# Probabilities of the last query blocks turned by VectorE and placed by way of DRAM

## The chip, the cores and the metric

The kernel runs on one core of a Trainium2 chip. The metric is the device time of one execution in microseconds (us). The kernel before took 1031.83 us (median of three runs, 1031.17 to 1034.34). Engines: PE is TensorE (matmuls; PEld its weight loads), DVE is VectorE, ACT is ScalarE, POOL is GpSimd, SP is SyncE, which here only issues DMAs.

## The reference

Decay attention (4 batches, 8 heads, 576 tokens, head dimension 64, float32), then two feed-forward blocks over the 2304 tokens:

```python
scores = scale * q @ k.T                      # per batch and head, 576 x 576
cum = cumsum(log(clip(f, 1e-4, 1)))
scores = where(causal, -1e9, scores + cum[:, None] - cum[None, :])
attn = exp(scores - max(scores)); attn = attn / (sum(attn) + 1e-9)
x = (attn @ v)  -> (2304, 512)
h = x @ w_in;  x = maximum(0.01 * h, h) @ w_out          # 512 -> 2048 -> 512
out = ((x @ w_a) * (x @ w_b)) @ w_out2                   # 512 -> 1536 -> 512
```

## The kernel before

Tokens are cut into 9 chunks of 256 (`x_chunk`). For each chunk the first feed-forward block runs as eight pieces of `l1` (line 865) and `l2` (line 895); float32 is carried as a rounded high part and a low part, so that a product is three matmul passes. The remaining stages (from some 620 us on) are not touched by the change.

Attention is cut into eight blocks: batch b, and r = 0 for queries 0 to 255 or r = 1 for queries 256 to 575 against all 576 keys. `att_steps` emits block n beside the feed-forward work of chunk n - 1, and `tc.high_priority` lets its PE instructions go up to 300 places ahead; a planner then orders every engine's queue from its own costs, and the order is fixed when the program is built. A block's eight heads go by pairs; head j = 0 or 1 of pair hp.

For one head of an r = 1 block, `att_scores` does this: SP loads queries, keys and `cumb` (the decay row); POOL writes the decay and the causal mask into the probability tiles `p` (lines 390, 393), one of 384 and one of 512 columns for the two tiles of 128 queries; PE computes scores; DVE adds them and finds the row's extreme (line 402); ACT takes the exponential (line 373) and multiplies by the reciprocal of the sum (line 411). The 64 last queries of both heads form a tile of their own, `p4`.

`att_values` then turns the probabilities over, since the product with v needs keys on the partitions: 3 + 4 PE transposes of 128x128 into PSUM (`pp`, line 99 stands for every PE instruction of attention, being the helper that records them) and two ACT copies (line 500) into the tile `pt`, which has one buffer and holds both heads of a pair. The tiles `p` have two buffers per tag. `att_rest` does the same for `p4` (lines 540, 541, 548), and `att_product` multiplies: for each key tile kt and head u,

```python
q_ = (P if kt == nkt - 1 else 0) if kt < nkt else T1
pe_att.matmul(av[u * 64 : u * 64 + 64, q_:width], vn[:, kt, u, :], turned[kt][:, u, q_:width] ...)
```

so that the last full key tile, which only the second 128 queries see, skips the first 128 columns. Then ACT and DVE bring the result as high and low part into the chunks' tiles `xh` and `xl` (`evac`, lines 456, 457). The v rows `vn` are loaded by SP (lines 481, 483). In blocks with r = 0 and in batch 0 the same functions run with other sizes. `first_block` does block (0, 0) in an order written out by hand.

Of the kernel before, what the change touches and what calls it, by code (L numbers as in the profile page):

```python
# [8 lines left out]
F32 = mybir.dt.float32  # L9
# [5 lines left out]
ALU = mybir.AluOpType  # L15
# [3 lines left out]
P = 128  # L19
MASKED = 1.0e9  # L20
ABOVE = 3.0e38
# [5 lines left out]
def kernel(  # L27
# [13 lines left out]
    nc = tc.nc  # L41
    B, H, S, D = q.shape
# [211 lines left out]
    def x_chunk(c):  # L254
        if c not in xh:
            pool, bufs = (late["p"], 1) if c % 3 == 2 else (mp, 2)
            xh[c] = pool.tile([P, HP, T1], F32R, tag="xh", bufs=bufs, name=f"xh_{c}")
            xl[c] = pool.tile([P, HP, T1], F32R, tag="xl", bufs=bufs, name=f"xl_{c}")
        return xh[c], xl[c]

    x4, p4s, stats, qks, turned_p, vhls, phs, lasts, lastk = ({} for _ in range(9))

    def att_scores(b, r, h, st):
# [50 lines left out]
        else:  # L314
# [50 lines left out]
            q_at = lead + z0  # L365
        cumb = ap_.tile([P, S], F32, tag="cumb", bufs=3, name=f"cumb_{nm}")
        made = nc.sync.dma_start(cumb[:, :nk], cum_dram[bh : bh + 1, :nk].to_broadcast([P, nk]))
        if b == 0:
# [11 lines left out]
            return rec  # L380

        ps = st["ps"] = {}
        for i in range(2):
            t = 2 * r + i
            n = (t + 1) * P
            s = 2 * j + i
            pt = ap_.tile([P, 384 if i == 0 else 512], F32, tag=f"p{i}", bufs=2, name=f"p_{nm}_{t}")[:, :n]
            ps[i] = pt

            made = pool_att.tensor_scalar(pt, cumb[:, :n], 1.0, ncum_t[:, t, bh : bh + 1], op0=ALU.mult, op1=ALU.add)  # L390
            if (b, r, h) == (0, 1, 0):
                tc.add_manual_dep(made.ins, quiet[0].ins.name, SYNC, reason="second block's decay behind the fourth pair")
            pool_att.affine_select(
                out=pt[:, t * P : n], in_=pt[:, t * P : n], pattern=[[-1, P]], base=0,
                channel_multiplier=1, compare_op=ALU.is_ge, fill=MASKED,
            )
# [5 lines left out]
            dve_att.tensor_tensor_reduce(  # L402
                out=pt, in0=sp[:, :n], in1=pt, op0=ALU.add, op1=ALU.min, scale=1.0, scalar=ABOVE,
                accum_out=stat[:, 0, s : s + 1],
            )
            yield
            exp(pt, s)
            yield
# [46 lines left out]
    def evac(hi, lo, src):  # L455
        high = act_att.copy(hi, src)
        return high, dve_att.tensor_tensor(out=lo, in0=src, in1=f32(hi), op=ALU.subtract)


    def turned_tile(name):  # L460

        t = ap_.tile([P, 2688], F32, tag="pt", name=f"pt_{name}")
        return [t[:, 640 * kt : 640 * kt + 640].rearrange("p (u q) -> p u q", u=2) for kt in range(4)] + [
            t[:, 2560:].rearrange("p (u q) -> p u q", u=2),
            t,
        ]

    def att_values(b, r, h, st):

        hp, j = h // 2, h % 2  # L470
        nk = 2 * P if r == 0 else S
        tok0 = b * S + (0 if r == 0 else 2 * P)
        nm = f"{b}_{r}_{h}"
        pair = (b, r, hp)
        ps = st["ps"]
        if j == 0:
            turned_p[pair] = turned_tile(nm)
            full, rest = nk // P, nk % P
# [7 lines left out]
        turned = turned_p[pair]  # L486
        yield
        parts = [([(kt, 0) for kt in range(2 * r + 1)], 0), ([(kt, 1) for kt in range(2 * r + 2)], 1)]
        if r == 0:
            parts = [([(0, 0), (0, 1), (1, 1)], None)]  # L490
        for z, (tiles, i) in enumerate(parts):
            pp = ps_a.tile([P, 4, P], F32, tag="ps", bufs=3, name=f"pp_{nm}_{z}")
            for m, (kt, i_) in enumerate(tiles):
                pe_att.transpose(pp[:, m, :], ps[i_][:, kt * P : kt * P + P], ident)
            if i is None:
                act_att.copy(turned[0][:, j, 0:T1], pp[:, 0:2, :].rearrange("p m q -> p (m q)"))
                st["second"] = act_att.copy(turned[1][:, j, P:T1], pp[:, 2, :])
            else:
                to = turned[5][:, :2560].rearrange("p (k u q) -> p k u q", k=4, u=2)
                st["second"] = act_att.copy(to[:, : len(tiles), j, i * P : i * P + P], pp[:, : len(tiles), :])  # L500
            yield
        if r == 0:
            yield
        if j == 1 and (r == 0 or b == 0):
            yield from att_product(b, r, hp, st["second"])

    def att_product(b, r, hp, ready):

        pair = (b, r, hp)
        nm = f"{b}_{r}_{2 * hp}"  # L510
        turned, vn = turned_p[pair], vhls[pair]
        tok0 = b * S + 2 * P * r
        width = 320 if r and b else T1
        nkt = 2 * r + 2
        av = ps_a.tile([P, width], F32, tag="ps", bufs=3, name=f"av_{nm}")
        for kt in range(nkt + (width > T1)):
            q_ = (P if kt == nkt - 1 else 0) if kt < nkt else T1
            for u in range(2):
                made = pe_att.matmul(
                    av[u * 64 : u * 64 + 64, q_:width], vn[:, kt, u, :], turned[kt][:, u, q_:width] if kt < 4 else turned[4][:, u, :],  # L520
                    start=(kt == 0), stop=(kt == nkt - (width == T1)),
                )
                if kt == u == 0:
                    tc.add_manual_dep(made.ins, ready.ins.name, SYNC, reason="both heads at once")
        p0 = 0
        while p0 < width:
            c = (tok0 + p0) // T1
            c0 = tok0 + p0 - c * T1
            n = min(width - p0, T1 - c0)
            ch, cl = x_chunk(c)  # L530
            evac(ch[:, hp, c0 : c0 + n], cl[:, hp, c0 : c0 + n], av[:, p0 : p0 + n])
            p0 += n
        yield

    def att_rest(b, hp, rec4):

        pair = (b, 1, hp)
        nm = f"{b}_1_{2 * hp}"
        turned, p4 = turned_p[pair], p4s[b, hp]
        act_att.mul(p4, p4, rec4)  # L540
        nc.gpsimd.memset(turned[5][64:, 2560:], 0.0)
        main = turned[5][:, :2560].rearrange("p (k u q) -> p k u q", k=4, u=2)[:, :, :, T1:320]
        tail = turned[5][:, 2560:].rearrange("p (k u q) -> p k u q", k=1, u=2)
        for k0, k1, w, to in ((4, 5, S - 4 * P, tail), (0, 4, P, main)):
            pp = ps_a.tile([P, 4, P], F32, tag="ps", bufs=3, name=f"pp{k1}_{nm}")
            for kt in range(k0, k1):
                pe_att.transpose(pp[:w, kt - k0, :], p4[:, kt * P : kt * P + w], ident)
            ready = act_att.copy(to[:w], pp[:w, : k1 - k0, :].rearrange("p k (u q) -> p k u q", u=2))
            yield
        yield from att_product(b, 1, hp, ready)  # L550

    def att_last(b, hp, rec4):
# [2 lines left out]
        vhl = vhls[b, 1, hp]  # L555

        p4 = p4s[b, hp]
        ph = turned_tile(f"4_{nm}")[5][:, :640].rearrange("p (k q) -> p k q", k=5)
# [63 lines left out]
    def first_block():  # L622
# [128 lines left out]
                )  # L751

        def probs(p, j, i):
            both = tile_of(
                ("p", p, j), lambda: ap_.tile([P, 384], F32, tag="qll" if p == 2 else f"p{j}", bufs=2, name=f"p_f{p}_{j}")
            )
            return both[:, i * P : i * P + (i + 1) * P]

        def D(p, j, i):
# [50 lines left out]
                pe.transpose(pp[:, z, :], probs(p, j, i)[:, kt * P : kt * P + P], ident)  # L810

        def h(p, j):
            pt = tile_of(("pt", p), lambda: turned_tile(f"f{p}")[5])
# [648 lines left out]
```

## Time and profile before

| | |
|---|---|
| median of 3 runs | 1031.83 us |
| the profiled execution | 1030.66 us |
| its span, first to last instruction | 1028.9 us |
| PE, DVE, ACT, POOL busy | 98%, 65%, 54%, 17% of the span |
| granted TensorE clock, mean | 0.992 |

The profile is one execution taken by the hardware profiler. Busy time is the union of an engine's instruction records; matmul records overlap, and their ends are modelled, so a matmul's cost is read from the distance of starts rather than from its length. The chain of waits follows the work that ended last back from instruction to instruction, through what released each.

### The profile page before, as it was taken

How to read it: one execution, taken by the hardware profiler on the slowest of the kernel's cores; microseconds unless marked ns; L12 is line 12 of the kernel's file. 1: busy time of each engine (PE TensorE's matmuls, PEld its weight loads, DVE VectorE, ACT ScalarE, POOL GpSimd, SP SyncE). 2: the span in 40 equal slices, each digit the busy share in tenths (PEclk: the TensorE clock that was granted, in tenths of full speed). 3: DMA queues.
4: the chain of work that ended last, by engine and by line, in shares of the span. 5: the costliest groups of instructions: out<-in, count | busy, mean ns of one | idle time of the engine just before them, and what ended most of it. 6: DMA issues, size and time to landing. Idle time of an engine off the chain costs nothing.

```text
span 1028.9 us, 19822 instructions
## 1 busy us (share of the span) xinstructions
PE 1005.5 (98%) x7299; PEld 913.8 (89%) x7299; DVE 671.6 (65%) x1383; ACT 557.9 (54%) x1144; POOL 178.4 (17%) x402
## 2 busy tenths in 40 slices
PE   6899999999999999999999999999999999899998
PEld 5677779999999999999999997888888888799998
DVE  5799656755626555264367547668686675898872
ACT  6688687986748867488455444232322222354430
POOL 3525325442413324133000000000000000000000
PEclk9899999999999999999999999999999999999999
DMA  8997145543532436321583123233151423757711
GB/s 218 270 266 217 48 96 110 106 93 62 112 78 62 92 62 110 80 55 45 188 298 119 62 62 103 94 122 118 57 164 41 159 100 125 238 150 203 212 53 42
DMA packets 230497, 125.78 MB, mean 122 GB/s; under 512 B 144704, under 2 KB 212160, under 8 KB 230400
## 3 DMA queue, kind: packets, MB, share of 16 engines
q1 hardware_dynamic: 224784, 118.67, 42.0%
q10 hardware_dynamic: 5616, 5.84, 1.7%
q8 instruction: 58, 0.95, 0.4%
q14 instruction: 39, 0.32, 0.1%
HBM read 95.29 MB, written 29.17 MB: 121 GB/s over the span
## 4 chain that ended last, share of the span: by engine, by line
PE 92%; DMA 4%; ACT 1%; DVE 1%; POOL 1%; issue 1%; SPq 0%; ACTq 0%; POOLq 0%; DVEq 0%
PE h L865 19%; PE y L895 19%; PE o L1200 12%; PE s L99 6%; PE b_b L1090 5%; PE b_a L1090 5%; PE av L99 5%; PE pp L99 4%; PE a_a L1090 3%; PE a_b L1090 3%; PE d_b L1090 3%; PE d_a L1090 3%; DMA homef<-in_moe_w_out_dram 2%; PE a_last L1122 2%; PE b_last L1122 2%; DMA homef<-o_dram 1%
## 5 line engine op out<-in xcount | busy, mean ns | idle before, releaser
L895 PE MATMUL y<-gh,homer 128*128 128x256 f32 x1152 | 227.2, 284 | 0.6 <-ACT gh L877 0.6
L865 PE MATMUL h<-xh,homer 128*128 128x256 f32 x1152 | 225.6, 283 | 0.9 <-ACT hs L878 0.9
L865 PEld LDWEIGHTS h<-xh,homer 128*128 128x128 f32 x1152 | 183.4, 188 | 5.6 <-issue 2.7
L895 PEld LDWEIGHTS y<-gh,homer 128*128 128x128 f32 x1152 | 183.8, 188 | 3.8 <-issue 2.1
L895 PE MATMUL y<-gl,homer 128*128 128x256 f32 x576 | 162.5, 284 | 0.0
L865 PE MATMUL h<-xl,homer 128*128 128x256 f32 x576 | 161.6, 281 | 0.0
L895 PEld LDWEIGHTS y<-gl,homer 128*128 128x128 f32 x576 | 108.4, 188 | 1.1 <-issue 0.9
L865 PEld LDWEIGHTS h<-xl,homer 128*128 128x128 f32 x576 | 108.3, 188 | 0.5
L390 POOL TENSOR_SCALAR p<-cumb,ncum_t 128x384 f32<-128x384 f32 (+2 forms) x112 | 75.7, 679 | 149.3 <-PE pp L99 86.3
L880 DVE TENSOR_TENSOR gl<-hs,gh 128x512 fp32r<-128x512 f32 x72 | 50.9, 707 | 71.9 <-ACT hs L878 71.3
L373 ACT ACTIVATE p<-p,stat 128x256 f32<-128x256 f32 (+3 forms) x123 | 73.6, 600 | 36.0 <-DVE stat L402 30.7
L402 DVE CUSTOM_DVE_ANT_0 p<-s,p 128x384 f32<-128x384 f32 (+2 forms) x100 | 48.4, 491 | 39.6 <-PE s L99 29.8
L877 ACT ACTIVATE gh<-h 128x512 fp32r<-128x512 f32 x72 | 42.7, 593 | 41.7 <-PE h L865 40.9
L411 ACT ACTIVATE p<-p,rec 128x384 f32<-128x384 f32 (+1 forms) x108 | 56.1, 572 | 11.5 <-DVE rec L379 10.6
L99 PE MATMUL pp<-ident,p 128*128 128x128 f32 (+1 forms) x376 | 62.2, 276 | 0.0
L1200 PE MATMUL o<-homer,homer 128*128 128x256 f32 x441 | 57.7, 284 | 0.0
L1200 PEld LDWEIGHTS o<-homer,homer 128*128 128x128 f32 x441 | 55.2, 191 | 0.2
L1200 PE MATMUL o<-w_o,homer 128*128 128x256 f32 x378 | 52.6, 284 | 1.4 <-ACT homer L933 1.4
L933 ACT CAST homer<-p 128x1536 fp32r<-128x1536 f32 (+1 forms) x26 | 33.7, 1320 | 35.3 <-DVE p L958 20.4
L1200 PEld LDWEIGHTS o<-w_o,homer 128*128 128x128 f32 x378 | 48.6, 191 | 2.1 <-ACT homer L933 1.8
L99 PEld LDWEIGHTS pp<-ident,p 128*128 128x128 f32 (+1 forms) x376 | 43.4, 139 | 4.0 <-issue 2.3
L99 PE MATMUL av<-pt,vn 128*64 128x320 f32 (+4 forms) x400 | 46.9, 372 | 0.0
(272 smaller groups left out, 2047.6 us busy)
## 6 DMA issues: line engine op xcount, KB each, us to landing
p<-p_dram SPq DMA_DIRECT2D x17, 768.0 KB, 6.6
p_dram<-p SPq DMA_DIRECT2D x12, 1024.0 KB, 4.3
cumb<-cum_dram SPq DMA_DIRECT2D x32, 288.0 KB, 3.9
homef<-in_moe_w_out_dram SPq DMA_DIRECT2D x15, 511.6 KB, 6.0
homef<-in_moe_w_in_dram SPq DMA_DIRECT2D x15, 510.5 KB, 4.7
raw_o<-in_moe_w_out_dram SPq DMA_DIRECT2D x12, 511.6 KB, 5.9
xq<-in_q_dram SPq DMA_DIRECT2D x144, 32.0 KB, 2.1
y_dram<-yo ACTq DMA_DIRECT2D x18, 256.0 KB, 2.9
```

The lines of the kernel that those rows point to most:

```text
L99: return method(*args, **kw)
L373: act_att.activation(pt, pt, AF.Exp, bias=stat[:, 0, s : s + 1], scale=-1.0, accum_out=stat[:, 1, s : s + 1])
L390: made = pool_att.tensor_scalar(pt, cumb[:, :n], 1.0, ncum_t[:, t, bh : bh + 1], op0=ALU.mult, op1=ALU.add)
L402: dve_att.tensor_tensor_reduce(out=pt, in0=sp[:, :n], in1=pt, op0=ALU.add, op1=ALU.min, scale=1.0, scalar=ABOVE, accum_out=stat[:, 0, s : ...
L411: act_att.mul(ps[i], ps[i], rec[:, i : i + 1])
L865: made = nc.tensor.matmul(hps[:, u, :], w[:, c * P : c * P + P], x[:, c, :], start=(n == 0), stop=(n == 3 * ND - 1))
L877: nc.scalar.activation(gh, hps, AF.Prelu, alpha=0.01)
L880: nc.vector.tensor_tensor(out=gl, in0=hs, in1=f32(gh), op=ALU.subtract)
L895: nc.tensor.matmul(o, w[:, d * P : d * P + P], g[:, u, :], start=(fi == 0 and n == 0 and d % 2 == 0), stop=(fi == NF1 - 1 and n == 2 and d ...
L1090: nc.tensor.matmul(to, w[:, W_ROWS[m], wl, c2 * P : c2 * P + P], y[c2][xl_][:, Y_COLS[m], :], start=(first and c2 == e == 0), stop=(c2 == ...
L1122: nc.tensor.matmul(ps[:, f * T1 : f * T1 + T1], w[:, wb, wl, c2 * P : c2 * P + P], y[:, xb, xl_, c2 * T1 : c2 * T1 + T1], start=(f == m == ...
L1200: nc.tensor.matmul(ps[m], xps[n, j // 3][:, X_ROWS[m], xl_, j % 3, :], wo2[j][:, O_COLS[m], wl, :], start=(j == e == y == 0), stop=(j == N ...
```

## The change

In blocks with b > 0 and r = 1 (`turns_by_dma`) PE's transposes and ACT's copies go. Both query tiles of a head share one tile `p` of 1024 columns, in which 32-column pieces of the first and the second tile alternate; POOL writes zeros where the first tile has no fourth key tile. One DVE instruction transposes every 32x32 block of it in place. Four DMAs on SP (one per 32 partitions) store it to a buffer in DRAM (`turn_dram`, one per parity of hp), in runs of 256 bytes; four DMAs load it from there into `pt` in runs of 1 KB, keys on the partitions. The queries come out regrouped: 32 of the first tile, 32 of the second, and so on. So the product's last full key tile covers all columns (zeros included), and `evac` picks its sources by 32s and writes each query tile and the 64 last queries apart. Elsewhere the tiles `p` of the two query tiles become one tile of 1024 columns with two buffers, `pt` is laid out head by head, and the two loads of the last v rows become one.

```diff
+    turn_dram = [dram.tile([32, 2, 4, 4, T1], F32, name=f"turn_{z}_dram") for z in range(2)]
+    VIA_DRAM = (0, 1)
+    def turns_by_dma(b, r, j):
+        return b > 0 and r == 1 and j in VIA_DRAM
...
+        both = ap_.tile([P, 1024], F32, tag="p", bufs=2, name=f"p_{nm}")
+        if turns_by_dma(b, r, j):
+            st["both"] = both
+            both = both.rearrange("p (c t k) -> p c t k", t=2, k=32)
+            pool_att.memset(both[:, 12:, 0, :], 0.0)
         for i in range(2):
...
-            pt = ap_.tile([P, 384 if i == 0 else 512], F32, tag=f"p{i}", bufs=2, name=f"p_{nm}_{t}")[:, :n]
+            if turns_by_dma(b, r, j):
+                blocks_of = lambda ap: ap.rearrange("p (c k) -> p c k", k=32)
+                pt, diagonal, pattern = both[:, : n // 32, i, :], both[:, 4 * t : 4 * t + 4, i, :], [[-32, 4], [-1, 32]]
+            else:
+                blocks_of = lambda ap: ap
+                pt = both[:, i * (n - P) : i * (n - P) + n]
+                diagonal, pattern = pt[:, t * P : n], [[-1, P]]
...
     def turned_tile(name):
         t = ap_.tile([P, 2688], F32, tag="pt", name=f"pt_{name}")
+        main, tail = t[:, :2560].rearrange("p (u k q) -> p u k q", u=2, k=4), t[:, 2560:].rearrange("p (u q) -> p u q", u=2)
+        return main, tail, t
...
-                if rest:
-                    nc.sync.dma_start(vs[:rest, full, u, :], v[b, h + u, full * P : nk, :])
             if rest:
+                nc.sync.dma_start(vs[:rest, full, :, :], v[b, h : h + 2, full * P : nk, :].rearrange("u p d -> p u d"))
...
+        if turns_by_dma(b, r, j):
+            both, turn = st["both"], turn_dram[hp % 2][:, j]
+            dve_att.transpose(out=both, in_=both)
+            for z in range(4):
+                nc.sync.dma_start(
+                    turn[..., 64 * z : 64 * z + 64].rearrange("j k b q -> j (k b) q"),
+                    both[32 * z : 32 * z + 32, :].rearrange("p (c q) -> p c q", c=16),
+                )
+            yield
+            for z in range(4):
+                nc.sync.dma_start(main[32 * z : 32 * z + 32, j, :, :T1], turn[:, :, z])
+            yield
+            return
...
-        for kt in range(nkt + (width > T1)):
-            q_ = (P if kt == nkt - 1 else 0) if kt < nkt else T1
+        wide = width > T1
+        for kt in range(nkt + wide):
+            q_ = T1 if kt == nkt else P if kt == nkt - 1 and not wide else 0
...
+        runs = [(0, T1, av)]
+        if wide:
+            tiles = av[:, :T1].rearrange("p (a t q) -> p t a q", t=2, q=32)
+            runs = [(t * P, t * P + P, tiles[:, t]) for t in range(2)] + [(T1, width, av[:, T1:].rearrange("p (a q) -> p a q", q=32))]
+        for p0, p1, src in runs:
+            while p0 < p1:
...
+                    evac(hi, lo, src[:, first_ : first_ + n // 32, :])
```

## Rows read from the trace of the kernel before

**Rows 1.** The page: engine, busy us (share of span) and instructions; the chain's shares.
```profile
PE 1005.5 (98%) x7299; PEld 913.8 (89%) x7299; DVE 671.6 (65%) x1383; ACT 557.9 (54%) x1144; POOL 178.4 (17%) x402
...
PE 92%; DMA 4%; ACT 1%; DVE 1%; POOL 1%; issue 1%; SPq 0%; ACTq 0%; POOLq 0%; DVEq 0%
```

**Rows 2.** Busy time by stretch: bounds, length; PE, PEld, DVE, ACT, POOL busy (instructions); clock.
```profile
160.00:510.00 350.00, 349.37 (x2909) 329.73 (x2908) 182.61 (x559) 252.09 (x631) 115.64 (x288) 1.00 0.39 86
```

**Rows 3.** Stretch 160 to 510 us: the chain by line; PE's waits (us, times, longest).
```profile
by line: PE h L865 33.7%; PE y L895 33.0%; PE s L99 11.1%; PE av L99 9.6%; PE pp L99 9.3%; DMA cumb<-cum_dram 2.1%; POOL p L418 0.6%; issue 0.5%; POOL p L393 0.1%; POOL p L390 0.1%; DVE stat L402 0.0%; POOL p L424 0.0%; POOL qhh L335 0.0%; 
...
PE s L99 <- DVE stat L402: 0.6, 1, 0.6
```

**Rows 4.** Timeline of PE from 449.9 us: start, length, line, operation, tiles, count.
```profile
449.95 2.28 PE L99 MATMUL av<-pt,vn 128*64 128x320 f32 x20
452.16 0.98 PE L99 MATMUL pp<-ident,p 128*128 128x128 f32 x7
452.90 0.38 PE L99 MATMUL s<-ks,qhh 128*128 128x288 f32 x1
453.12 0.30 PE L99 MATMUL s<-ks,qll 128*128 128x288 f32 x1
```

**Rows 5.** Instruction groups by shape, 160 to 510 us: busy us, mean ns; idle before.
```profile
L99 PE MATMUL av<-pt,vn 128*64 128x192 f32 x48 | 5.9, 326 | 0.0
```

**Rows 6.** The same view, DVE's transpositions.
```profile
L326 DVE STREAM_TRANSPOSE tq<-xq 128x320 f32<-128x320 f32 x24 | 12.2, 510 | 0.6
...
L350 DVE STREAM_TRANSPOSE tk<-xk 128x576 f32<-128x576 f32 x11 | 8.3, 756 | 0.0
```

**Rows 7.** The same view, the copy out of PSUM and the low part's subtraction.
```profile
L500 ACT COPY pt<-pp 128x512 f32<-128x512 f32 x24 | 14.1, 588 | 0.4 <-PE pp L99 0.4
...
L457 DVE TENSOR_TENSOR xl<-av,xh 128x128 fp32r<-128x128 f32 x16 | 4.5, 290 | 11.5 <-ACT xh L456 11.4
```

**Rows 8.** Timeline of ACT, POOL and PE around two pairs' ends.
```profile
355.62 1.24 ACT L411 ACTIVATE p<-p,rec 128x384 f32<-128x384 f32 x2
...
367.68 1.03 PE L99 MATMUL av<-pt,vn 128*64 128x320 f32 x6
...
462.22 1.23 ACT L411 ACTIVATE p<-p,rec 128x384 f32<-128x384 f32 x2
...
466.61 2.28 PE L99 MATMUL av<-pt,vn 128*64 128x320 f32 x20
...
468.75 1.23 ACT L411 ACTIVATE p<-p,rec 128x384 f32<-128x384 f32 x2 [0.49 <-DVE rec L379]
...
469.53 1.27 POOL L390 TENSOR_SCALAR p<-cumb,ncum_t 128x384 f32<-128x384 f32 x2
...
483.91 2.28 PE L99 MATMUL av<-pt,vn 128*64 128x320 f32 x20
```

**Rows 9.** DMAs: issue on SP (ns, min/median/max), landing; KB and median landing.
```profile
L481 SPq DMA_DIRECT2D vn<-in_v_dram x56: 368/462/1138, 41.2 to 470.3; - x56
...
DMA to landing us min/median/max: 1.9/2.4/6.4
...
vn<-in_v_dram SPq DMA_DIRECT2D x32, 128.0 KB, 2.5
ty<-y_dram SPq DMA_DIRECT2D x16, 256.0 KB, 3.0
...
vn<-in_v_dram SPq DMA_DIRECT2D x24, 64.0 KB, 2.1
```

**Rows 10.** Timeline of SP, first and last of 22 issues of one pair.
```profile
198.28 0.38 SPq L481 DMA_DIRECT2D vn<-in_v_dram  x1
...
209.11 0.42 SPq L345 DMA_DIRECT2D xk<-in_k_dram  x1
```

**Rows 11.** Batch 3's last product (timeline); the `h` matmuls issued before 524.25 us.
```profile
497.33 2.28 PE L99 MATMUL av<-pt,vn 128*64 128x320 f32 x20
...
L865 PE MATMUL h<-xh,homer x896: 274/280/390, 44.1 to 524.2; 128*128 128x256 f32 x180
```

More of the change, by code (lines that the diff above doesn't have):

```diff
@@ L363, in score @@
                 pe_att.matmul(o, qll[:, c0 : c0 + P], ks[:, cols_], start=False, stop=True)
[L365 removed]
+            q_at = 2 * z0
         cumb = ap_.tile([P, S], F32, tag="cumb", bufs=3, name=f"cumb_{nm}")
@@ L386, in att_scores @@
             s = 2 * j + i
-            pt = ap_.tile([P, 384 if i == 0 else 512], F32, tag=f"p{i}", bufs=2, name=f"p_{nm}_{t}")[:, :n]
+            if turns_by_dma(b, r, j):
[5 more added lines that the diff above has]
+                diagonal, pattern = pt[:, t * P : n], [[-1, P]]
             ps[i] = pt
-            made = pool_att.tensor_scalar(pt, cumb[:, :n], 1.0, ncum_t[:, t, bh : bh + 1], op0=ALU.mult, op1=ALU.add)
+            made = pool_att.tensor_scalar(
+                pt, blocks_of(cumb[:, :n]), 1.0, ncum_t[:, t, bh : bh + 1], op0=ALU.mult, op1=ALU.add
+            )
             if (b, r, h) == (0, 1, 0):
@@ L393, in att_scores @@
             pool_att.affine_select(
-                out=pt[:, t * P : n], in_=pt[:, t * P : n], pattern=[[-1, P]], base=0,
+                out=diagonal, in_=diagonal, pattern=pattern, base=0,
                 channel_multiplier=1, compare_op=ALU.is_ge, fill=MASKED,
@@ L402, in att_scores @@
             dve_att.tensor_tensor_reduce(
-                out=pt, in0=sp[:, :n], in1=pt, op0=ALU.add, op1=ALU.min, scale=1.0, scalar=ABOVE,
+                out=pt, in0=blocks_of(sp[:, :n]), in1=pt, op0=ALU.add, op1=ALU.min, scale=1.0, scalar=ABOVE,
                 accum_out=stat[:, 0, s : s + 1],
@@ L490, in att_values @@
             parts = [([(0, 0), (0, 1), (1, 1)], None)]
+        if mixed:
+            ordered = main[:, j, :, :T1].rearrange("p k (z t q) -> p k z t q", z=4, t=2)
+            nc.gpsimd.memset(ordered[:, 3, :, 0, :], 0.0)
         for z, (tiles, i) in enumerate(parts):
@@ L510, in att_product @@
         nm = f"{b}_{r}_{2 * hp}"
-        turned, vn = turned_p[pair], vhls[pair]
+        (main, tail, _), vn = turned_p[pair], vhls[pair]
         tok0 = b * S + 2 * P * r
@@ L524, in att_product @@
                     tc.add_manual_dep(made.ins, ready.ins.name, SYNC, reason="both heads at once")
[L525 to L532, printed above, removed]
+        runs = [(0, T1, av)]
[4 more added lines that the diff above has]
+            while p0 < p1:
+                c = (tok0 + p0) // T1
+                c0 = tok0 + p0 - c * T1
+                n = min(p1 - p0, T1 - c0)
+                hi, lo = (x[:, hp, c0 : c0 + n] for x in x_chunk(c))
+                if wide:
+                    first_ = (p0 % P) // 32
+                    hi, lo = (x.rearrange("p (a q) -> p a q", q=32) for x in (hi, lo))
+                    evac(hi, lo, src[:, first_ : first_ + n // 32, :])
+                else:
+                    evac(hi, lo, src[:, p0 : p0 + n])
+                p0 += n
         yield
@@ L540, in att_rest @@
         act_att.mul(p4, p4, rec4)
[L541 to L544, printed above, removed]
+        nc.gpsimd.memset(turned[2][64:, 2560:], 0.0)
+        for k0, k1, w, to in (
+            (4, 5, S - 4 * P, turned[1].rearrange("p u (k q) -> p k u q", k=1)),
+            (0, 4, P, turned[0][..., T1:320].rearrange("p u k q -> p k u q")),
+        ):
             pp = ps_a.tile([P, 4, P], F32, tag="ps", bufs=3, name=f"pp{k1}_{nm}")
@@ L753, in probs @@
         def probs(p, j, i):
-            both = tile_of(
-                ("p", p, j), lambda: ap_.tile([P, 384], F32, tag="qll" if p == 2 else f"p{j}", bufs=2, name=f"p_f{p}_{j}")
-            )
+            if p == 2:
+                both = tile_of(("p", p, j), lambda: ap_.tile([P, 384], F32, tag="qll", bufs=2, name=f"p_f{p}_{j}"))
+            else:
+                both = tile_of(("p", p), lambda: ap_.tile([P, 1024], F32, tag="p", bufs=2, name=f"p_f{p}"))
+                both = both[:, j * 512 : j * 512 + 384]
             return both[:, i * P : i * P + (i + 1) * P]
```

27 lines of the change are left out of this document (14 added, 13 removed).

## The prediction

> **What bounds the kernel now.** I read the busy table and the chain of waits first [rows 1]. TensorE (PE) is busy 1005.5 of 1028.9 us and the chain that ended last runs on it for 92% of the span: what leaves PE's queue leaves the time, as long as nothing makes PE wait in its place. Since shares of busy time are averages over stages, I looked at the stretch that the change edits, the attention of batches 1 to 3. There PE is busy 349.37 of 350 us at a granted clock of 1.00, while VectorE (DVE) has 183 us of work, ScalarE (ACT) 252 and GpSimd (POOL) 116 [rows 2]. Its own chain says what that PE time is: two thirds MoE matmuls, 9.3% the `pp` transposes; and 2.1% of it passes through the transfer of `cumb`, which ends in the one PE wait of the stretch, 0.6 us [rows 3]. So attention runs beside MoE work, which fills PE, and a transpose costs exactly its own PE time.
>
> **What is removed from PE.** A head has 3 + 4 transposes in `att_values`; with 8 heads and 3 batches that is 168. The matmul records (270 ns) overlap, so I don't multiply by them. Seven transposes start at 452.16 and the next matmul at 452.90, with a record longer than its like by 0.08: 0.82 us, 0.118 each [rows 4]. Over the whole stretch the chain gives 9.3% of 350 us, 32.6 us, to 288 transposes, 0.113 each [rows 3]. I take the mean over many, 0.113: 168 x 0.113 = 19.0 us (0.118 gives 19.8).
>
> A rule of the Trainium skill speaks against the change: VectorE: DVE Perf Modes, "Rules for kernel authors", wants a 128x128 transpose on TensorE when its result may lie in PSUM, as here; the same page's "The three transpose paths" gives it 390 ns. By that figure 65 us would leave PE and the sum would be about 970 us, an estimate; the rows show the pitch, and the pitch decides.
>
> **What is added to PE.** With queries regrouped, the product's fourth key tile can no longer skip its first 128 columns: 192 columns become 320. A pair's product is 20 matmuls, 2.21 us [rows 4]: 12 of 320 columns, 4 of 192 [rows 5], 4 of 64, 4864 columns, 0.45 ns each. 4 x 128 more make 0.23 us, for 12 pairs 2.8 us.
>
> **What is added elsewhere.** DVE: the transposition of 128x1024 a head. Rows of 320 and 576 elements took 510 and 756 ns [rows 6], 0.96 ns an element, so 1.18 us, and 24 heads 28.4 us on an engine with 183 of 350 us in use: it hides. ACT loses two copies a head, of 512 columns (588 ns [rows 7]) and of 384, some 25 us in all. The results now leave PSUM in 4, 3 and 4 pieces a pair (batches 1, 2, 3) instead of 2: 20 more copies and subtractions, about 0.29 us each [rows 7], 6 us on ACT and on DVE, not in front of PE. POOL gets a small memset a head. The probabilities' two halves now share a buffer, so the first half comes free only with the second, half a microsecond later than now (four of the seven transposes of [rows 4]).
>
> **The way through DRAM, beside the path.** Per head: 1.2 us DVE, four stores, four loads. The nearest row to a store of 128 KB in runs of 256 B is the load of `vn`, same size and runs: 0.46 us of SP each and 2.5 us to landing; to the reload (runs of 1 KB) it is `ty`, 3.0 us [rows 9]. Stores: 3 x 0.46 + 2.5 = 3.9; reloads: 3 x 0.46 + 3.0 = 4.4; together 9.5 us. Bounds: 8 us if all land in the 1.9 us of the quickest, 17 if in the 6.4 us of the slowest [rows 9]. I take 9.5, by the rows of the same size and runs.
>
> What hides it? In the pair whose second head is normalised by 469.98 (468.75 + 1.23), the product starts at 483.91, 13.9 us later, since the 64 last queries go through scores, exponential and their own transposes meanwhile [rows 8]. So the second head's reload has 4.4 us to spare; in the shortest of the twelve pairs (356.86 to 367.68) it has 1.3. At the upper bound of 17 us PE would wait 3.1 us or more in each of twelve products, 37 us. The first head, done by 463.45, lets go of its buffer at 469.53 now, and would after its stores at 463.45 + 5.1 = 468.6 [rows 8]; its reload must wait for the product of the pair before (466.61 to 468.8), because `pt` has one buffer, and then stands in SP's queue ahead of the next pair's loads. The cadence of 16.7 us a pair survives.
>
> A second rule of the skill, DMA: Bandwidth & Descriptors, "Specifications", has transfers below 512 B done as read-modify-write. No run here shows it for stores. Were it to double the data time (2.5 less 2.1 us for 64 KB more in [rows 9], so 0.8 a store), four stores would take 3.2 us more: 12.7 us, still under 13.9 and the sum unchanged, but over the shortest pair's 10.8. It adds a little to the first rival's chance.
>
> **SP's queue** is the tight place. A loaded pair has 22 issues from 198.28 to 209.53 [rows 10], 9.9 us by their durations. The change adds 16 and takes 1 away (`vs` in one transfer instead of two): 15 x 0.46 = 6.9, so 16.8 us in a pair of 16.7. In SP's queue every load stands behind a store that waits for DVE, or a reload that waits 2.5 us for the stores to land. But there is room: only the first three pairs of a block carry the next heads' loads, and the results are needed late. The last product of batch 3 ends at 499.6, and the first chunk that reads it starts with the L865 matmuls after 524.2 (by then 896 = 7 chunks x 128 of the `xh` kind are issued) [rows 11]: 24.7 us, 19 once the block's own PE work shrinks by 5.7.
>
> **Sum.** 1030.66 (the profiled execution; 1.2 us under the median of the runs, so within their scatter) - 19.0 + 2.8 = 1014.5. For twelve new places where PE can wait I add 1.5 us, between none and twelve times the 0.6 us of the one wait that PE has there now [rows 3]. 1016 us.
>
> **Rivals.**
> 1. SP falls behind and PE waits for the products (slower). If nothing fills the two landing waits of a pair, SP needs 16.8 + 5.0 = 21.8 us for 16.7: 5.1 late a pair, piling up over the three loaded pairs of a block, less the spare 4.4: 10.9 us of PE standing still at the last product, in the blocks of batches 1 and 2 (batch 3 has few loads left): 1016 + 21.8 = 1038. It decides from 14.5 us of waiting in all, 1.2 a product. For it: SP is full already, the chain's 2.1% through `cumb`. Against: 24.7 us of slack behind a block, loads that can run in the landing waits.
> 2. PE's order is fixed ahead by the planner. Where it counts on a shorter way through DRAM than 9.5 us, products stand too early in PE's queue, every one of them. At 1 us each, twelve take 12 us: 1028, within 0.3% of before. For it: no row shows what the planner takes a transfer to cost, and a PE without idle time has no cover against its errors. Against: the 4.4 us to spare.
> 3. Nothing is gained because PE had idle time there: excluded by 349.37 of 350 us [rows 2].
>
> **Chances.** Forecast 0.66 (1009 to 1022); rival 2 at 0.15 (1022 to 1031); rival 1 at 0.18 (1031 and more); 0.01 below. A measurement of this kernel tells about 0.3%, 3.1 us, from no change. Faster by more: 0.66, 0.01 and half of rival 2, 0.74; within: 0.08; slower: 0.18. The range 1009 to 1036 leaves out rival 1's upper part.
>
> **What would show it.** PE has 168 `pp` instructions fewer, and no products of 192 columns. PE stays at full in 160 to 500, and attention's last product lies some 15 us earlier than 497.3 or a little less. Right: no idle time of PE before `av`; stores land 2 to 3 us after issue. Wrong: PE waits for `pt` from a DMA, in the products of batches 1 and 2 more than in batch 3 (rival 1) or in all alike (rival 2); SP's queue without gaps; `cumb` waited for by POOL for longer.

## The result and the profile after

The changed kernel takes 1047.16 us (median of 4 runs) against 1031.92 beside it: ratio 1.0148, 95% interval 1.012 to 1.0177. It is slower by some 1.5%, and outside the predicted range. The first profiled execution took 1050.55 us, a second one 1043.66.

The page of the changed kernel, as in [rows 1]: busy time, the busiest DMA queue, and the chain.

```profile
PE 1004.7 (96%) x7131; PEld 904.6 (86%) x7131; DVE 698.6 (67%) x1427; ACT 538.7 (51%) x1116; POOL 176.7 (17%) x426
...
q1 hardware_dynamic: 289040, 143.85, 52.7%
...
PE 71%; DMA 10%; SPq 7%; ACT 3%; issue 3%; DVE 3%; POOL 2%; POOLq 0%; ACTq 0%; DVEq 0%
```

The 168 transposes are gone (7299 to 7131 matmuls), but the chain has left PE: 92% to 71%, with 10% DMA and 7% SP's queue (SPq) in it. The same stretch as [rows 2] and the head of its chain, as [rows 3]:

```profile
160.00:510.00 350.00, 335.81 (x2686) 309.87 (x2685) 209.85 (x611) 232.60 (x615) 120.57 (x326) 1.00 0.70 147
```

```profile
by line: PE h L917 17.5%; PE y L947 16.1%; PE s L100 6.3%; PE av L100 6.2%; SPq L329 5.1%; DMA xk<-in_k_dram 4.9%; DMA turn_dram<-p 4.5%; issue 4.3%; SPq L512 3.8%; SPq L518 2.9%; DMA pt<-turn_dram 2.8%; SPq L352 2.3%; ACT p L432 1.8%; POOL
```

PE is idle for 14 of 350 us where it was idle for 0.6, and DMA's share (next to last in the row) went from 0.39 to 0.70. The chain now passes through the stores (L512), the reloads (L518), and also through the loads of queries (L329) and keys (L352) behind them in SP's queue. PE's waits in the attention of batches 1 to 3 (us in total, times, longest):

```profile
PE av L100 <- DMA pt<-turn_dram: 5.1, 4, 2.7
PE s L100 <- DVE stat L423: 4.1, 6, 1.6
PE y L947 <- ACT gh L929: 1.8, 1, 1.8
PE s L100 <- ACT qhh L344: 1.6, 1, 1.6
```

Only a third is products waiting for `pt`; the scores wait too. Queries and keys come late: VectorE, which transposes them, waits for their loads (140 to 560 us), as it never did before:

```profile
DVE tq L333 <- DMA xq<-in_q_dram: 13.3, 12, 3.0
DVE tk L357 <- DMA xk<-in_k_dram: 7.9, 7, 2.0
```

SP's queue shows why (start, length, issues); from 245 to 270 us no two of its rows are more than 0.2 us apart:

```profile
245.03 2.19 SPq L518 DMA_DIRECT2D pt<-turn_dram  x3
247.26 0.92 SPq L329 DMA_DIRECT2D xq<-in_q_dram  x2
248.22 0.45 SPq L352 DMA_DIRECT2D xk<-in_k_dram  x1
248.78 2.26 SPq L512 DMA_DIRECT2D turn_dram<-p  x4
251.09 1.89 SPq L352 DMA_DIRECT2D xk<-in_k_dram  x3
...
254.12 1.74 SPq L518 DMA_DIRECT2D pt<-turn_dram  x4
255.97 2.45 SPq L512 DMA_DIRECT2D turn_dram<-p  x4
258.45 2.04 SPq L329 DMA_DIRECT2D xq<-in_q_dram  x3
```

Stores and reloads stand between the loads, four and four, at 0.44 to 0.73 us each; they land a little later than the 2.5 and 3.0 us of the prediction (issue to landing, median):

```profile
turn_dram<-p SPq DMA_DIRECT2D x96, 128.0 KB, 3.0
pt<-turn_dram SPq DMA_DIRECT2D x96, 128.0 KB, 3.2
```

**A ruler.** To compare stages I use the first `h` matmul of each chunk: from chunk 1 to chunk 7 (or 8) lies all attention of batches 1 to 3. Before, that is 140.0 to 524.3: 384.2 us (431.6 to chunk 8). After: 392.5 and 391.8 in the two executions (439.9 and 439.7). So the stage lost 8 us instead of gaining 15. Where distances between successive starts of matmuls exceed 0.33 us, I add up what exceeds 0.12 ("excess"): 2.0 us before, 20.5 and 20.8 after. The granted clock matters to this ruler: in the stage the records have it at 0.5 (1.2 GHz) for no time in the kernel before and in the first execution of the changed one, but for 6.8 us in the second. The rest of the difference in the first pair of profiled executions, 12 us, lies ahead of chunk 1, which starts at 152.0 instead of 140.0.

### The profile page after: what moved, and what is told of

It is laid out like the page before. It is cut to its first block, busy times and chain, and to the rows that moved or that the text cites. A ratio compares the mean times of both kernels' runs of the same rounds, so it can differ in the third digit from the quotient of the medians.

```text
span 1048.8 us, 19858 instructions
## 1 busy us (share of the span) xinstructions
PE 1004.7 (96%) x7131; PEld 904.6 (86%) x7131; DVE 698.6 (67%) x1427; ACT 538.7 (51%) x1116; POOL 176.7 (17%) x426
## 4 chain that ended last, share of the span: by engine, by line
PE 71%; DMA 10%; SPq 7%; ACT 3%; issue 3%; DVE 3%; POOL 2%; POOLq 0%; ACTq 0%; DVEq 0%
PE h L917 13%; PE y L947 13%; PE o L1252 12%; PE b_b L1142 5%; PE b_a L1142 5%; PE s L100 3%; PE a_a L1142 3%; PE a_b L1142 3%; PE d_b L1142 3%; PE d_a L1142 3%; PE av L100 3%; DMA turn_dram<-p 2%; SPq L329 2%; DMA homef<-in_moe_w_out_dram 2%; DMA xk<-in_k_dram 2%
## 5 line engine op out<-in xcount | busy, mean ns | idle before, releaser
L409 POOL TENSOR_SCALAR p<-cumb,ncum_t 128x384 f32<-128x384 f32 (+1 forms) x112 | 75.8, 686 | 133.4 <-ACT kn L311 43.7
L100 PE MATMUL av<-pt,vn 128*64 128x320 f32 (+3 forms) x400 | 54.1, 377 | 6.9 <-DMA pt<-turn_dram 5.1
L100 PEld LDWEIGHTS av<-pt,vn 128*64 128x64 f32 x400 | 30.0, 136 | 26.0 <-issue 6.9
L100 PE MATMUL s<-ks,qhh 128*128 128x288 f32 (+4 forms) x144 | 45.7, 327 | 6.0 <-DVE stat L423 4.2
L423 DVE CUSTOM_DVE_ANT_1 p<-s,p 128x384 f32<-128x384 f32 (+1 forms) x48 | 28.9, 616 | 26.3 <-POOL p L414 12.4
## 6 DMA issues: line engine op xcount, KB each, us to landing
turn_dram<-p SPq DMA_DIRECT2D x96, 128.0 KB, 3.0
pt<-turn_dram SPq DMA_DIRECT2D x96, 128.0 KB, 3.2
```

Of the source, the lines that this page charges most:

```text
L100: return method(*args, **kw)
L409: made = pool_att.tensor_scalar(pt, blocks_of(cumb[:, :n]), 1.0, ncum_t[:, t, bh : bh + 1], op0=ALU.mult, op1=ALU.add)
L423: dve_att.tensor_tensor_reduce(out=pt, in0=blocks_of(sp[:, :n]), in1=pt, op0=ALU.add, op1=ALU.min, scale=1.0, scalar=ABOVE, accum_out=stat ...
```

## The experiments

The ratio of each kernel is to the kernel before run beside it; the chunk columns are of one profiled execution.

| kernel | chunk 1 at | 1 to 7 | 1 to 8 | median us | ratio (95%) |
|---|---|---|---|---|---|
| before | 140.0 | 384.2 | 431.6 | 1031.92 | |
| the change | 152.0 | 392.5 | 439.9 | 1047.16 | 1.0148 (1.012 to 1.0177) |
| after_again | 144.2 | 391.8 | 439.7 | 1046.33 | 1.0145 (1.0095 to 1.0196) |
| pe_turn | 139.0 | 386.2 | 434.2 | 1035.34 | 1.0024 (0.9998 to 1.0049) |
| shared_p | 147.8 | 383.5 | 430.9 | 1037.14 | 1.0027 (1.0 to 1.0053) |
| one_v | 143.3 | 385.0 | 432.4 | 1031.69 | 0.9989 (0.9964 to 1.0015) |
| second_only | 139.7 | 384.9 | 439.6 | 1042.37 | 1.0075 (1.0048 to 1.0101) |
| no_route | 139.8 | 372.0 | 419.9 | 1021.18 | 0.989 (0.9859 to 0.9921) |
| issue_paced | 142.4 | 412.9 | 461.3 | 1066.32 | 1.0345 (1.0289 to 1.04) |
| no_landing | 139.4 | 395.6 | 443.4 | 1045.65 | 1.0107 (1.007 to 1.0144) |
| stores_act | 142.3 | 385.2 | 433.0 | 1037.42 | 1.0027 (1.0001 to 1.0054) |
| joint_reload | 145.1 | 402.0 | 450.0 | 1055.99 | 1.0225 (1.0168 to 1.0281) |
| second_act | 146.2 | 381.9 | 429.7 | 1036.82 | 1.0038 (1.0006 to 1.0071) |
| act_pool | 149.6 | 381.8 | 429.1 | 1035.26 | 1.0025 (1.0004 to 1.0047) |
| late_head_first | 146.5 | 387.4 | 434.8 | 1039.93 | 1.0061 (1.0036 to 1.0086) |
| stores_act_late | 144.2 | 383.1 | 430.8 | 1034.31 | 1.0021 (0.9999 to 1.0042) |
| act_pool_late | 146.8 | 377.6 | 422.8 | 1028.27 | 0.9962 (0.994 to 0.9983) |

### Is it the way through DRAM, and what happens before chunk 1?

**pe_turn**: `VIA_DRAM = ()`. **second_only**: `VIA_DRAM = (1,)`. **shared_p** and **one_v** are the kernel before with one line of the change each: `tag="p"` with 1024 columns, and

```diff
+                nc.sync.dma_start(vs[:rest, full, :, :], v[b, h : h + 2, full * P : nk, :].rearrange("u p d -> p u d"))
```

> The change with the way through DRAM left out: PE transposes all heads again, ACT copies, and all the rest of the change stays (shared tile p of 1024 columns, one load of the last v rows, regrouped queries, the product over all 320 columns). In the trace of the changed kernel chunk 1 of the feed-forward block starts at 152.0 us instead of 140.0, before any block that goes by DRAM has begun. Theory A: two separate losses. The first 12 us come from the parts that also act in batch 0 (shared tile or joined load), so they stay here: chunk 1 starts near 152, and 1032 + 12 + 2.8 (wider product) = about 1047 us. Theory B: the first 12 us belong to the way through DRAM or to one odd execution: chunk 1 starts near 140 and the time is about 1035 us. In the blocks r = 1 the distance of the chunks is that of before plus about 1 us under both.

> The kernel before with one edit of the change alone: the probabilities of a head's two query tiles in one tile of 1024 columns instead of two tiles (384 and 512). Theory A1 (the first half of a buffer comes free only with the second, which delays POOL's decay and with it the loads behind it in SP's queue): about 1044 us, chunk 1 near 152. Theory A2 (the joined load of the last v rows is at fault): about 1032 us, chunk 1 near 140.

> The kernel before with one edit of the change alone: the two DMAs of the last v rows joined into one. Theory A2 (one DMA fewer in SP's queue makes the planner place the start stage otherwise, so that SP stands behind the load of the decay row and the feed-forward weights come late): about 1044 us, chunk 1 near 152. Theory A1 (the shared tile is at fault): about 1032 us, chunk 1 near 140.

> The change with the way through DRAM for the second head of a pair alone; PE transposes the first head. Eight more DMAs on SP a pair instead of sixteen: 15 x 0.46 less 8 x 0.46 = 3.2 us of issue, 13 us of issue in a pair of 16.7, and one landing wait of about 3 us. Theory A (SP's queue is what lets the products wait): it nearly keeps up, the waits for pt fall from some 24 us to under 5, PE loses 84 transposes (9.5 us): if the first 12 us stay, about 1047 - 9.5 + 4 = 1041 us, otherwise about 1029. Rival (the planner puts the products too early for the way through DRAM, whatever SP has to do): the second head is the late one, so each product waits as now, and the time is about 1050 us or more.

> The changed kernel once more, unaltered. Its profiled execution had chunk 1 start at 152.0 us; kernels with the same order of the queues up to there had it at 139.0 to 145.1. Theory A (the start stage differs from one execution to the next, by how the first loads and conversions meet, and this one was a late one): another execution has chunk 1 between 139 and 146, the distance from chunk 1 to chunk 7 stays 392.5 within 2, and the profiled time is 1035 to 1044. Theory B (something in the changed kernel delays the start each time): chunk 1 at 150 or later again, and 1046 or more.

Without the way the stage takes 386.2 us, 2.0 more than before, the wider product's share: the loss in the stage belongs to the way. VectorE doesn't wait for queries or keys there. Theory A of the start stage fell with pe_turn (chunk 1 at 139.0) and again with after_again (144.2): in a second execution of the same program 8 of the 12 us were gone. All profiled kernels made from the changed one, issue_only (told below) apart, share the order of PE's and SP's queues up to some 180 us, and have chunk 1 anywhere from 139.0 to 152.0. shared_p was late (147.8) with an order of its own.

The records show what the late start consists of. From the first `h` matmul of chunk 0 to that of chunk 1 the first execution of the changed kernel took 111.9 us, the kernel before 96.0. PE was idle for 9.6 us of it against 2.1, and the granted clock was at 0.5 (1.2 GHz) for 20.5 us against 3.4. If PE's work takes twice as long at half the clock, this makes 7.5 + 8.5 = 16.0 us, an estimate, for a difference of 15.9. The worst part, before and after (the clock is the third number from the end):

```profile
60.00:90.00 30.00, 28.94 (x202) 22.38 (x201) 29.17 (x62) 27.52 (x51) 13.22 (x15) 1.00 0.89 265
60.00:90.00 30.00, 25.33 (x120) 19.99 (x122) 21.21 (x40) 20.86 (x38) 4.38 (x6) 0.72 0.75 212
```

In the four runs with chunk 1 at 139.0 to 139.8 no record between the two chunks is at 0.5; in the five with it at 146.5 to 152.0 it is at 0.5 for 10.2 to 23.9 us. Why the waits and the clock differ so from run to run, and whether the changed kernel is late more often than others (its two medians are 13 and 15 us above the kernel before, where the stage explains 8), stays open.

second_only has the stage at 384.9 and then loses 7 us after chunk 7 (439.6 to chunk 8): there `h` waits 5.2 us for ACT, which stands behind a late landing of `y_dram`. By the stage to chunk 7 theory A held (no product waits for `pt`). The whole time, 1042.37 us, is neither A's (1029, as the start was early here) nor the rival's (1050 or more); I count it undecided.

### What would the change be worth with the way for free?

**no_route** writes DVE's result straight into `pt`:

```diff
-            dve_att.transpose(out=both, in_=both)
...
-                nc.sync.dma_start(main[32 * z : 32 * z + 32, j, :, :T1], turn[:, :, z])
+            for z in range(4):
+                dve_att.transpose(out=main[:, j, z, :T1], in_=both[:, z * T1 : z * T1 + T1])
```

> The changed kernel with no store and no reload: DVE transposes the 32x32 blocks straight into pt (four instructions a head), so the keys stand on the wrong partitions and the products are of other numbers; PE, ACT, POOL and the wider product are as in the changed kernel, SP has 16 DMAs a pair fewer. It shows what the change would be worth if the way through DRAM were free. By the distance of starts in the traces (168 transposes at 0.087 us, 14.7 us, less 1.9 for the wider product) chunk 1 to chunk 7 takes 384.2 - 14.7 + 1.9 = 371.4 us and the time is about 1034 - 13 = 1021. By the prediction's 0.113 each it is 367 and 1017. If waits stay although SP is relieved (the planner's order is at fault), it is 380 or more, and 1030 or more.

1021.18 us, 372.0 in the stage, PE busy again:

```profile
160.00:510.00 350.00, 346.40 (x2842) 323.58 (x2841) 222.17 (x691) 235.36 (x613) 118.67 (x316) 1.00 0.40 92
```

The gain is there, 12.2 us in the stage. The expectation's working was off though its sum was not: less excess (5.8 us here, 2.0 before) the stage went from 382.2 to 366.1, so 16.1; with 12 x 0.21 for the wider product (2.21 to 2.42) the transposes were worth 18.6 us, 0.111 each. 0.087 counts only the distance from each transpose to the next start; by it the 168 were worth 14.7 us. Where the other 4 us come from, or whether they belong to the excess that I took out, isn't shown. The way costs 392.5 - 372.0 = 20.5 us.

### Issue time, landing waits, or the length of the way?

**issue_paced** (pe_turn, with four idle stores behind each of the four ACT copies of a pair), **no_landing** (`else_` is a view of the queries in DRAM), **stores_act** (the four stores) and **joint_reload**, in this order:

```diff
...
+                    made = nc.sync.dma_start(
+                        turn_dram[16 * (b - 1) + 4 * hp + 2 * j + z][y // 2, y % 2], ident[sl, None, :64].to_broadcast([32, 16, 64])
+                    )
+                    tc.add_manual_dep(made.ins, st["second"].ins.name, SYNC, reason="paced")
...
-                nc.sync.dma_start(main[32 * z : 32 * z + 32, j, :, :T1], turn[:, :, z])
+                nc.sync.dma_start(main[32 * z : 32 * z + 32, j, :, :T1], else_[:, j, :, z])
...
-                nc.sync.dma_start(
+                nc.scalar.dma_start(
...
-            for z in range(4):
-                nc.sync.dma_start(main[32 * z : 32 * z + 32, j, :, :T1], turn[:, :, z])
+            for z in range(4 * j):
+                nc.sync.dma_start(
+                    main[32 * z : 32 * z + 32, :, :, :T1].rearrange("i j k q -> i (j k) q"),
+                    turn_dram[hp % 2][:, :, :, z].rearrange("i j k q -> i (j k) q"),
+                )
```

> The change with the way through DRAM left out (PE transposes all heads), and in its place 16 idle stores of 128 KB a pair on SP, in runs of 256 bytes, that nothing waits for and that wait for nothing. Theory T1 (SP's time to issue is what costs: its queue is full, queries and keys come late): the distance from the first matmul of chunk 1 to that of chunk 7, 386.2 us without these stores, grows by 10 us or more, and the time is 1045 us or more. Theory T2 (what costs is that SP stands at the stores and reloads, waiting for DVE, for the landing and for the buffer pt, with other loads behind): the distance stays within 3 us of 386, the time 1033 to 1038.

> The change without the way through DRAM (PE transposes all heads), and with 16 idle stores a pair on SP, 128 KB in runs of 256 bytes, four behind each ACT copy of transposed probabilities; they wait for that copy, and nothing waits for them. T1 (SP's time to issue is what costs): loads behind them come late, PE waits for queries and scores: the distance from chunk 1 to chunk 7 grows from 386.2 to 396 or more (the changed kernel has 18 us of such stretches), and the time is 1043 or more. T2 (the length of the way through DRAM): 386 to 389 us, 1034 to 1038.

> The changed kernel, except that the reload takes its 128 KB from the queries in DRAM and not from the stored probabilities, in the same shape and runs; the stores stay, but nothing waits for their landing (the products are of other numbers). T1 (time to issue): as many issues as in the changed kernel, so nothing changes but the 11 us for which SP waited for landings: 1042 to 1047 us, chunks 1 to 7 within 3 us of 392.5. T2 (the waits inside SP's queue, and the length of the way): the largest of them and PE's waits for pt go: 381 to 385 us from chunk 1 to chunk 7, 1030 to 1036 in all. Under the rival that the planner counts on a shorter way than there is, PE's waits in front of the products go too, and those for queries (s behind DVE and ACT) stay.

> The changed kernel with the four stores of each head issued by ACT instead of SP: SP keeps 8 of the 16 added issues and no longer waits for DVE's transposition; ACT, with some 257 of 390 us in use, gets 96 issues. T1 (SP's time to issue): SP is back at about 13 us a pair, and PE's waits go with it: 384 us or less from chunk 1 to chunk 7, 1030 to 1036 in all. T2 (landing waits in SP's queue): they stay at the reloads, so half or more of the loss stays: 388 us or more, 1040 or more. If ACT itself then waits for DVE in front of copies that PE needs, PE waits for ACT (pp, s and y behind ACT), and the time is 1045 or more.

> The changed kernel with both heads of a pair loaded back by four DMAs of 256 KB after the second head's stores, instead of four of 128 KB a head: 12 DMAs a pair instead of 16, and SP stands at one reload a pair instead of two, the first head's no longer ahead of the second head's loads. T1: 1.8 of the 7 us of added issue go, so about a quarter of the loss: 390 us from chunk 1 to chunk 7, some 1043 in all. T2: half of the landing waits and the early wait for pt go: 386 us or less, 1038 or less; PE's wait for pt in front of products may grow, since both heads now come last (up to 1 us in each of twelve).

**issue_only** (the idle stores waiting for nothing) met T1's bounds, but told nothing between the theories: the queue got the stores in bulk ahead of feed-forward weights, for which PE then waited up to 24.3 us at once, and once 43.0 us for ACT; it took 1158.59 us. It shows what issues cost back to back, 0.68 us each:

```profile
239.37 12.26 SPq L528 DMA_DIRECT2D turn_dram<-ident  x18
```

issue_paced tells most: with no reload, no landing wait and all transposes on PE, 16 idle issues a pair cost 26.7 us in the stage (386.2 to 412.9), more than the whole way. PE waits for scores, whose queries and keys come late (VectorE waits 20.3 and 15.2 us for them), and once 6.1 us for the copies; the clock was at 0.5 for 13.7 us of the stage:

```profile
PE s L100 <- DVE stat L423: 8.0, 5, 4.3
PE pp L100 <- ACT pt L535: 6.1, 1, 6.1
PE pp L100 <- ACT p L432: 2.9, 3, 1.1
```

These stores also move as many bytes as the changed kernel's stores and reloads, so SP's issues and their DMA traffic are one in this run. act_pool_late (below) parts them: with the same bytes as the changed kernel and nearly the same DMA share (0.69 from 160 to 510 us, against 0.70) its stage takes 377.6, so the traffic alone isn't the cause.

```profile
160.00:510.00 350.00, 345.64 (x2809) 323.35 (x2810) 218.35 (x621) 234.43 (x623) 172.90 (x416) 1.00 0.69 150
```

no_landing says the same as issue_paced from the other side: SP no longer waits for landings, PE hardly for `pt` (0.5 us), and the stage takes 395.6, no less than the changed kernel's 392.5 (10.2 us of it at a clock of 0.5, which can account for some 5 of them). In stores_act the bytes stay, SP waits longer for landings than in the changed kernel (first line), and only eight issues a pair leave SP: 385.2, 7.3 us back.

```profile
SPq L518 <- DMA turn_dram<-p: 11.4, 11, 2.9
...
SPq L518 <- DMA turn_dram<-p: 40.7, 28, 5.7
```

T2's range fell in issue_paced and no_landing, while no_landing is 0.1 us outside T1's; stores_act lies between the bounds, 1.2 us above T1's and 2.8 below T2's. T1 is the better account. joint_reload, with a quarter fewer issues, came out by neither theory, worse by 9.5 us: both heads' rows now come after the second head's stores, and PE waits for products up to 5 us at a time. So the way's length does count once the reload is moved to the end.

The scores could also be late because POOL gets the buffers `p` back only when the stores have landed: VectorE waits 21.6 us for POOL's decay (160 to 545 us) where it waited 6.7 before (160 to 510). But in act_pool_late it waits 25.9 us for it, and PE's wait for the scores is only 0.7.

### Where is the rest?

stores_act still lacks 13 us to no_route. **second_act** is stores_act for the second head alone; **stores_pool**, **all_pool** and **act_pool** give stores, both, or the reloads alone (stores on ACT) to `nc.gpsimd`.

> The changed kernel with only the second head of each pair by way of DRAM, its four stores issued by ACT; SP has four added issues a pair, ACT four. T1: SP has room, so PE's waits fall to about 2 us, PE saves 84 transposes (7.3 us) less 1.9: 380 us from chunk 1 to chunk 7, 1030 us in all, some 4 us better than before. T2 (landing waits and the length of the way): waits of 7 us as with the second head's stores on SP: 385 us, 1035 or more.

> The changed kernel with the four stores of each head issued by POOL instead of SP. POOL has some 125 of 390 us in use between 140 and 530 us; no run has shown what one issue costs it. If the rest of the loss with the stores on ACT (385.2 us from chunk 1 to chunk 7, against 372.0 without the way) is ACT's issue time (some 96 issues of up to 0.68 us), it goes: about 376 us, 1026 in all. If it is the eight reloads on SP with their landing waits, it stays: 384 to 387, 1036. If an issue costs POOL 1 us or more, POOL falls behind with the decay and PE waits for scores: 395 or more.

> The changed kernel with the stores and the reloads of each head issued by POOL; SP has the work it has without the way. If SP is the only cause: 372 to 376 us from chunk 1 to chunk 7, 1022 to 1026 in all. If the length of the way or POOL's standing at the landing waits costs (the decay of the next heads comes late): 385 or more, 1036 or more.

> The changed kernel with the stores issued by ACT and the reloads by POOL; SP has the work it has without the way. If the rest of the loss lies in SP's eight reloads: 374 to 378 us from chunk 1 to chunk 7, 1024 to 1030 in all. If it lies in ACT's issue time: 383 to 387, about 1036. If POOL at the landing waits makes the decay late: more than 387.

second_act is between its two theories: 381.9 in the stage, but 1036.82 in all. Stores on POOL cost 1156.47 us, stores and reloads 1243.72: a store every 2.9 us, with nothing that the profile shows in between:

```profile
242.74 0.66 POOL L512 DMA_DIRECT2D turn_dram<-p  x1 [2.90 <-issue]
245.63 0.65 POOL L512 DMA_DIRECT2D turn_dram<-p  x1 [2.23 <-issue]
248.47 0.66 POOL L512 DMA_DIRECT2D turn_dram<-p  x1 [2.20 <-issue]
```

Reloads on POOL go four in 2.21 us, so act_pool does what it should: SP issues no more than without the way, and PE's excess falls to 7.2 us. And yet the stage takes 381.8. What is left is in the product. From act_pool's timeline of PE (start, length, tiles, count):

```profile
235.89 0.75 PE L100 MATMUL av<-pt,vn 128*64 128x320 f32 x2
236.57 0.39 PE L917 MATMUL h<-xh,homer 128*128 128x256 f32 x1
236.79 0.28 PE L917 MATMUL h<-xl,homer 128*128 128x256 f32 x1
237.00 2.48 PE L100 MATMUL av<-pt,vn 128*64 128x320 f32 x18
```

The two heads' matmuls write different halves of `av` and start 7 ns apart when they stand side by side: 20 records in 2.42 us (no_route, pe_turn). Here the first head's first matmul stands alone, 0.68 us for its two records, and the other 18 still take 2.41. Its wait is for its own head's reload, so it could be placed early; the second head's waits for the later reload. In act_pool 11 of 12 products are split so; in the changed kernel 6 appear in two pieces of 2 and 18 records, and one more in four pieces. The guard of the kernel before, "both heads at once", hangs the first matmul on ACT's last copy, which no longer covers the second head.

**late_head_first**, **stores_act_late**, **act_pool_late**: the second head's matmul first, which is released last.

```diff
-            for u in range(2):
+            for u in (1, 0) if wide else (0, 1):
...
-                if kt == u == 0:
+                if kt == 0 and u == wide:
```

> The changed kernel, with one edit: in the product of the blocks r = 1 the second head's matmul stands before the first head's, for every key tile. If the split of the product is a loss of its own, the pieces of 2 and 18 records become one of 20 and 2.42 us, 0.68 us less for each product that is split in the changed kernel (9 to 12 of 12): chunk 1 to chunk 7 in 384 to 386 us instead of 392, about 1040 in all. If the time is lost to SP alone, later heads only wait longer in front of the product: 391 or more, 1046.

> The same edit, with the stores issued by ACT and the reloads left on SP. If the split is the rest of the loss: about 379 us from chunk 1 to chunk 7 instead of 385.2 (4 us of waits stay with SP), 1031 in all. If SP's eight reloads are the rest: 384 or more, 1036.

> The same edit, with the stores issued by ACT and the reloads by POOL. If the split is the rest of the loss: the products' 47.2 us fall to 40, and chunk 1 to chunk 7 takes 373 to 376 us instead of 381.8, 1027 to 1030 in all, which is better than the kernel before by some 5 us. If the rest is the length of the way or ACT's issue time, it stays at 380 or more, 1034 or more.

All 12 products are whole in all three:

```profile
233.76 2.49 PE L100 MATMUL av<-pt,vn 128*64 128x320 f32 x20
```

That is act_pool_late. In the changed kernel the edit gives 5.1 us of the stage (6 x 0.68 = 4.1 and the one in four pieces; I expected 6 to 8), although 6.8 us of the stage now ran at a clock of 0.5, as in after_again; in act_pool 4.2 to chunk 7 and 6.3 to chunk 8 (11 x 0.68 = 7.5), in stores_act only 2.1: there waits grew from 11.9 to 13.8 us of excess, between the two ranges that I had expected and nearer to that for SP's eight reloads as its rest. act_pool_late, at 1028.27 us, is faster than both kernels: ratio 0.9962 to the kernel before, interval 0.994 to 0.9983.

## Why the prediction was wrong

- **PE's saving** (19.0 us) was about right: 18.6 by no_route with the excess taken out, 14.7 by the transposes' own distances of 0.087. The Trainium skill, VectorE: DVE Perf Modes, "The three transpose paths", gives 390 ns for one transpose in bfloat16; here, in float32 and in a full queue, it was 0.087 to 0.111 us. **The wider product** (2.8): 12 x 0.21 = 2.5.
- **DVE, ACT, POOL beside the path**: right as to size (the 128x1024 transposition is 1.24 us against 1.18), and no engine became the bound.
- **Landing** (2 to 3 us): 3.0 and 3.2, a little more. What the Trainium skill, DMA: Bandwidth & Descriptors, "Specifications", says of pieces under 512 B got no test by itself; the stores in runs of 256 bytes landed no later than the reloads in runs of 1 KB.
- **The failed step is SP's queue**: "But there is room", with slack behind a block and loads that run in the landing waits, and "the cadence of 16.7 us a pair survives". I worked out 16.8 us of issue for 16.7 of time and then entered 1.5 us of waits. The price of an issue was right (median 0.50 us for a store and 0.43 for a reload, against 0.46); what a full queue does to the loads in it was put at next to nothing. The room behind a block is of no use to the scores inside it: their queries and keys are loaded by the same queue one pair ahead, and behind the added issues they come late: VectorE waits 21.2 us for queries and keys where it waited for none before, and 3.2 in act_pool_late, where SP is relieved. From 275 to 340 us SP's pieces add up to 56.1 of 65 us (112 DMAs) where they were 34.9 (68 DMAs) in the same stretch before. The excess is 20.5 us where I added 1.5 to the 2.0 of before.
- **Rival 1** had the place and the order of size. Batches 1, 2, 3 (chunks 1 to 3, 3 to 5, 5 to 7) took 140.8, 134.9, 116.8 us against 128.9, 128.0, 115.1 without the way: 11.9, 6.9 and 1.7 lost, least in batch 3, as it said. Its mechanism was half right: issue time rather than landing waits (no_landing), and mostly late loads rather than products.
- **Rival 2** (products too early in PE's queue) is not shown as a cost of its own: PE's waits for `pt` are 5.1 us, and they came with SP's load; in act_pool_late, with the same way, they are 1.9.
- **Missed altogether**: the split product, some 5 us. I had listed for the new wait what it waits for, not that two instructions which run at once now had two different releasers.
- **Outside the stage**: 4 to 12 us of the start stage in the two profiled executions, where I had put nothing. It consists of PE's waits and of a lower granted clock; one execution of each kernel can't price it, and what sets it off is open.

So of the 20.5 us that the way costs: 5.1 by the split (late_head_first), 9.9 by SP (387.4 to 377.6 when all issues of the way leave it), and 5.6 left against no_route (2.9 to chunk 8), not taken apart further. The first two are rough: late_head_first had 6.8 us of the stage at a clock of 0.5, the executions on either side of it none, so up to 3.4 us may belong to the split instead of SP. By the medians of the whole time, start stage included, the split is worth 6.4 to 7.2 us and SP 11.7.

## What to carry to other kernels

Price a DMA by its time in the issuing queue first: where that queue's issues fill the period, one more set delays every load behind it, however well its own landing is hidden, and slack at the end of a block doesn't help the loads inside it. When instructions that run at once get their operands by different ways, let the one that is released last stand first. And time the change with its costly part left out (here no_route) before refining it: that tells what there is to win.

## What the runs showed of the hardware

- Issuing a 128 KB store in runs of 256 bytes took 0.68 us on SP back to back (18 in 12.26), on ACT 2.74 us for four in a row (stores_act; 0.37 each by the median of its 96), and on POOL 2.9 us from one to the next, though a reload in runs of 1 KB took POOL 0.55.
- Two matmuls on different halves of the output's partitions took 0.54 us together in the product (no_route: four records, starts 7, 262, 7 and 262 ns apart; the first pair 0.59), and the first head's alone 0.68 (act_pool).
- After a wait of PE the granted clock can fall, and then a wait costs more than its length. In after_again PE waited 2.2 us for DVE ahead of 205.3; the records have the clock at 0.5 (1.2 GHz) from 205.1 to 211.9, and the product there, its first matmul alone, took 5.7 us instead of 2.4:

```profile
203.00:212.00 9.00, 6.82 (x24) 3.44 (x23) 4.88 (x11) 2.98 (x7) 3.85 (x9) 0.62 0.71 168
```

```profile
205.31 0.61 PE L100 MATMUL s<-ks,qhh 128*128 128x288 f32 x1 [2.16 <-DVE stat L423]
...
206.56 5.77 PE L100 MATMUL av<-pt,vn 128*64 128x320 f32 x20
```
